# Attention and feed-forward on one core: the list that orders casts, copies, loads, score pieces and feed-forward pieces, written anew

## The chip, the cores and the metric

The kernel runs on one core of one Trainium2 chip. The metric is the time of one execution on the device in microseconds (us), as a median over runs. The profiled execution is a run of its own and has its own time.

## The reference

There are two steps. The first is masked attention for 4 batches, 8 heads, 768 tokens and head size 64. The second is a feed-forward layer on its output.

```python
B, H, S, D = q.shape                      # 4, 8, 768, 64
scores = matmul(q, k.T) / sqrt(D)         # per batch and head
# heads 0, 2, 6 ("retrieval"): causal mask
# heads 1, 3, 4, 5, 7 ("streaming"): causal and (key < 4 or query - key < 64)
a = softmax(where(mask, scores, -1e9)); attn = matmul(a, v)
x = attn.transpose(0, 2, 1, 3).reshape(3072, 512)
h = x @ w_in                              # 512 -> 2048
g = maximum(h, 0) + alpha * minimum(h, 0)
out = g @ w_out                           # 2048 -> 512, float32
```

## The kernel before, in words

The attention is cut into 16 segments n, four to a batch; segment n holds batch n // 4 and the head pair PAIRS[n % 4] of (2, 6), (1, 5), (0, 4), (3, 7). The feed-forward layer is cut into 8 token tiles t, two to a batch: even t has 512 tokens, odd t 256. The feed-forward tiles of batch b need the four segments of that batch, so the kernel alternates: attention of batch 0, feed-forward of tiles 0 and 1 with the attention of batch 1 woven in, and so on.

The order of all work is written out by hand. `ORDER` is a string of 1,076 names; each name is an item, a small function that emits its instructions, and a loop at line 806 calls them in the order of the string. A framework adds the semaphore waits that the data needs, but it moves nothing: every engine and every DMA queue carries out its own instructions strictly in the order in which the string emits them. The names are

- `Lq5`, `Lk5`, `Lv5`: the loads of q, k, v for segment 5, all on the queue of SyncE (SP) except the first half of `Lk0` (ScalarE's queue) and two small pieces of `Lk13` (GpSimd's). One load of a segment is 384 to 448 KB. `load_rows` (line 230) reads v in rows of 256 bytes. Up to segment 7, q comes in rows of 1,536 bytes and k in rows of 512 or 1,536; from segment 8 on both come in rows of 256. The buffers qf, kf, vf have four slots each, so that a load waits for the cast of the segment four before it.
- `wi0` to `wi7` (line 690) and `wo0` to `wo3` (line 695): the loads of w_in (eight pieces) and w_out (four pieces of 1 MB in the source), on GpSimd's queue, which converts them to bf16 on the way.
- `Cq6`, `Ck6.0`, `Cv6`: casts of a loaded tile to bf16. Which engine makes one is fixed by three strings, lines 296 to 298: GpSimd ("P") for v of segments 0 to 5, VectorE ("V") from segment 6 on (both halves of `Cv3` stand apart). `Cv6` is emitted by `cast_v` (line 346, its instruction is at line 348 and writes vb).
- `Tq`, `Tk`, `tq`, `tk`: transposes of q and k on TensorE (to segment 7) and the copies out of PSUM; `Dq`, `Dk`: the same by DMA transpose on SP's queue (from segment 8).
- `S4.0.3`, `s4.0.3`, `m4.0.3`: one piece of the scores on TensorE, its exponential on ScalarE, its mask on VectorE. From segment 4 on, score pieces that follow each other with nothing but light items between them are collected and emitted as one group by `emit_burst`; where both heads of a group have at least 576 columns, the two heads run side by side on the two halves of the array.
- `A4.0`, `a4.0`: scores times v on TensorE and the division on VectorE; `X4`, `x4`: the transpose into xT (by DMA on SP's queue for segments 4 to 14).
- `P0.9` (`P1`, line 588): one piece of x @ w_in in one PSUM bank; `p0.9` (`relu`, line 600) is its negative part on ScalarE into one of three buffers; `g0.9` (`prelu`, line 604) combines the two on VectorE and gives the bank free. `P0.0.0` to `P0.5.2` are the first six pieces of tile 0, cut in three by head pair.
- `O0.1.2`, `o0.1`: a quarter of g @ w_out, and the copy and store of the result (`P2_out`, line 620); `L0` to `L2`, `l0` to `l2`: the last 128 tokens, cut by columns.
- `warm0` to `warm8`: matmuls on a tile of zeros, whose result nobody reads; `busy`, `zero`, `kz`, `qz`, `vz`, `sz`, `so`, `ro`, `nz`, `kfz`, `near`: fills; `id`, `nms`, `nmr`, `nr`, `ns`: the identity and the masks, made on GpSimd.

PSUM has eight banks. An item on TensorE takes one (two for early scores) and the item that reads it last gives it back; `take` (line 144) picks the bank that has been free longest in the order of the string, so the string fixes which item waits for which.

Of the kernel before, what the change touches and what calls it, by code (L numbers as in the profile page):

```python
# [24 lines left out]
p1.12 P0.14 g1.12 p0.14 g0.14 P0.13 p0.13 g0.13 P0.11 p1.14 Tk5 Ck7.1 g1.14 P1.10 tk5.0 p0.11 p1.10 Ck6.0 Ck7.0 g0.11  # L25
m8.0.2 tk5.1 wo2 Lv6 Lv4 P0.10 P0.8 p0.8 Tk7 g1.10 wo3 Cq4 Lk9 P0.12 P1.8 p0.10 g0.8 p0.12 g0.10 Tq4 P0.6 P0.9 p0.3
Ck6.1 g0.3 tq4 P0.4.0 P0.5.0 Tk6 P0.4.1 p1.8 g1.8 tk7.0 p0.9 g0.9 Cq6 P0.5.1 P0.5.2 p0.5 g0.12 p0.6 tk6.1 P0.4.2 g0.6
g0.5 tk6.0 S4.0.5 P0.7 p0.7 P1.6 g0.7 P1.4 s4.0.5 p0.4 Tq6 m4.1.2 tk7.1 g0.4 Cv5 p1.6 g1.6 O0.1.0 tq6 S4.0.3 O0.2.0
O0.2.1 S5.1.1 S5.0.0 S4.0.1 S6.1.0 m14.0.2 p1.4 g1.4 s5.0.0 O0.1.1 s4.0.3 s4.0.1 O0.2.2 S5.0.2 S5.1.0 S4.0.2 S5.1.2
s6.1.0 m4.0.1 Cv7 O0.3.0 s5.0.2 s5.1.2 s5.1.1 s4.0.2 O0.1.2 s5.1.0 O0.1.3 o0.1 Cq7 Cv4 O0.3.1 m5.1.0 m8.1.2 m5.0.2  # L30
m4.0.3 m5.1.2 S4.0.0 S4.1.4 S5.0.1 S4.0.4 S4.1.0 s4.0.4 s5.0.1 Lk10 m5.0.1 O0.2.3 O0.3.2 Tq7 m5.0.0 o0.2 s4.1.0 m4.0.4
m5.1.1 A5.1 s4.0.0 m4.0.0 a5.1 O0.3.3 tq7 S7.0.0 S7.0.1 S4.1.3 S7.1.1 S6.0.5 S4.1.1 m4.0.5 s4.1.4 o0.3 Lq9 s4.1.3 Ck8
m4.1.3 A5.0 a5.0 X5 s4.1.1 A4.0 s7.0.0 s7.1.1 Lk11 Lq8 s7.0.1 a4.0 s6.0.5 near1 m7.0.0 m7.1.1 m4.1.0 O1.1.0 S7.1.0
S6.0.4 S7.0.2 S4.1.5 S6.0.1 S7.1.2 S6.1.1 O1.1.1 Cv6 s7.1.0 O1.0.0 s4.1.5 m7.0.1 s6.1.1 m4.1.5 m6.1.1 s7.1.2 m6.1.0
# [812 lines left out]
```

## Time and profile before

| | |
|---|---|
| median of 3 runs | 229.18 us (229.06 to 229.55) |
| the profiled execution | 229.83 us, span 228.0 us |
| TensorE busy | 222.4 us, 98% of the span |
| VectorE, ScalarE, GpSimd busy | 151.6, 139.6, 45.8 us |
| DMA packets | 95,417; 82,440 of them under 512 bytes |
| first and last matmul start | 1.07 and 224.87 us |

The span runs from the first to the last instruction of the program on the core; 1.83 us of the execution lie around it. All times inside the kernel are counted from the span's start. Among the groups of instructions, each matmul of the feed-forward layer is listed with a modelled length (326 and 379 ns in the mean); what one costs is read from the distance between starts in the time line, 0.216 us for 512 columns and 0.109 us for 256.

### The profile page before, as it was taken

The page shows a single profiled execution, that of the slowest core. Times are in us where ns is not written, and L with a number is a line of the kernel's source. Part 1 is how long each engine was busy: PE and PEld are TensorE (multiplying, and loading weights), DVE is VectorE, ACT ScalarE, POOL GpSimd, SP SyncE. Part 2 cuts the span into 40 slices and gives each one's busy share as a digit, 9 for nine tenths or more (in the row PEclk, how much of TensorE's full clock was granted, in tenths as well). Part 3 has the DMA queues.
Part 4 walks back from the last instruction along what each step waited for, and adds up shares of the span by engine and source line. Part 5 has one row for each costly group of instructions (what it writes and reads, how often), then busy time and mean ns, then how long its engine had stood idle before and what let it go on. Part 6 is the DMA issues. An engine that isn't in the chain of part 4 may idle for free.

```text
span 228.0 us, 5239 instructions
## 1 busy us (share of the span) xinstructions
PE 222.4 (98%) x2005; PEld 135.9 (60%) x2005; DVE 151.6 (66%) x395; ACT 139.6 (61%) x284; POOL 45.8 (20%) x91
## 2 busy tenths in 40 slices
...
DMA  6999999999998798989969899995821420000213
GB/s 190 313 229 210 286 223 262 206 197 241 206 287 142 132 204 227 172 192 181 254 153 199 194 266 146 218 166 107 132 93 38 116 95 0 0 4 0 88 66 123
DMA packets 95417, 37.39 MB, mean 164 GB/s; under 512 B 82440, under 2 KB 93600, under 8 KB 95392
## 3 DMA queue, kind: packets, MB, share of 16 engines
...
q14 instruction: 10, 0.08, 0.2%
...
## 4 chain that ended last, share of the span: by engine, by line
PE 92%; ACT 3%; DVE 2%; issue 1%; DVEq 0%; ACTq 0%
PE P L597 35%; PE P L617 34%; PE P L552 7%; PE P L430 4%; PE P L687 3%; PE P L413 2%; PE P L363 2%; PE P L636 2%; ACT neg L602 1%; PE P L501 1%; DVE kT L392 1%; PE P L423 1%; PE P L577 1%; ACT kT L392 1%; ACT eS L523 1%
## 5 line engine op out<-in xcount | busy, mean ns | idle before, releaser
L609 DVE SCALAR_TENSOR_TENSOR g<-neg,oma,P 128x256 bf16<-128x256 f32 (+1 forms) x128 | 71.0, 608 | 35.9 <-ACT neg L602 35.5
L597 PE MATMUL P<-xT,w_in_b 128*128 128x512 bf16 (+1 forms) x512 | 86.5, 326 | 0.0
L617 PE MATMUL P<-w_out_b,g 128*128 128x512 bf16 x368 | 85.4, 379 | 0.0
L602 ACT ACTIVATE neg<-P 128x512 f32<-128x512 f32 x96 | 54.4, 600 | 27.2 <-PE P L597 22.6
L597 PEld LDWEIGHTS <-w_in_b 128*128 128x128 bf16 x512 | 49.5, 98 | 31.7 <-DVE g L609 0.2
L617 PEld LDWEIGHTS <-g 128*128 128x128 bf16 x368 | 33.8, 98 | 37.2 <-issue 1.2
L469 ACT ACTIVATE eR<-P 128x448 bf16<-128x448 f32 (+4 forms) x63 | 37.1, 636 | 5.4 <-PE P L430 2.3
L623 ACT COPY ot<-P 128x512 f32<-128x512 f32 x23 | 13.8, 602 | 37.8 <-PE P L617 32.9
L627 POOL DMA_DIRECT2D out_dram<-ot x18 | 10.3, 571 | 113.2 <-ACT ot L623 113.0
L517 ACT ACTIVATE eS<-P 128x352 bf16<-128x352 f32 x45 | 21.0, 493 | 3.7 <-PE P L430 3.7
L563 DVE TENSOR_TENSOR xn<-P,rcp 128x448 bf16<-128x448 f32 (+1 forms) x32 | 19.5, 608 | 1.1
L528 DVE TENSOR_TENSOR eS<-eS,ms_near 128x352 bf16<-128x352 bf16 x45 | 14.3, 334 | 4.4 <-ACT eS L517 4.2
L479 DVE TENSOR_TENSOR eR<-eR,mr_near 128x128 bf16<-128x128 bf16 (+5 forms) x54 | 12.1, 252 | 4.0 <-ACT eR L469 4.0
L430 PE MATMUL P<-qT,kT 64*128 64x176 bf16 (+13 forms) x181 | 11.7, 251 | 0.3 <-DVE g L609 0.3
L430 PEld LDWEIGHTS <-kT 64*128 64x128 bf16 x181 | 7.2, 94 | 7.6 <-issue 6.8
L413 PE MATMUL P<-qT,kT 128*128 128x192 bf16 (+14 forms) x68 | 11.3, 251 | 0.3 <-ACT eS L523 0.3
L552 PE MATMUL P<-vb,eS 128*128 128x65 bf16 x260 | 11.0, 193 | 0.4 <-DVE eS L528 0.4
L552 PEld LDWEIGHTS <-eS 128*128 128x128 bf16 x260 | 9.7, 97 | 2.9 <-DVE eS L528 0.6
L562 DVE RECIPROCAL rcp<-P 128x7 f32<-128x7 f32 (+1 forms) x32 | 6.3, 198 | 7.1 <-PE P L552 6.9
L552 PE MATMUL P<-vb,eR 128*128 128x65 bf16 x276 | 10.1, 192 | 0.0
L552 PEld LDWEIGHTS <-eR 128*128 128x128 bf16 x276 | 9.4, 97 | 1.2
L645 DVE COPY ot<-P 128x128 f32<-128x128 f32 x1 | 0.3, 292 | 14.3 <-PE P L636 14.3
...
## 6 DMA issues: line engine op xcount, KB each, us to landing
...
w_out_b<-in_moe_w_out_dram POOLq DMA_DIRECT2D x4, 512.0 KB, 13.4
```

The costliest lines, as they stand in the source:

```text
L413: nc.tensor.matmul(to, keys, queries, start=True, stop=stop)
L430: nc.tensor.matmul(to, keys[own], queries[own], start=True, stop=True)
L469: nc.scalar.activation(ebuf[n, hh][:, lo:hi].rearrange("p (x c) -> p x c", x=len(parts)), P[:, got[0]:got[0] + len(parts), 0:(hi - lo) // ...
L517: nc.scalar.activation(slots, sc[:, 0:352].rearrange("p (s c) -> p s c", c=176), AF.Exp, scale=scale)
L528: nc.vector.tensor_tensor(slots, slots, ms_near[:, 0:2, :] if m == 0 else ms_near[:, 1:3, :], op=ALU.mult)
L552: nc.tensor.matmul(pav[:, i, :], e[:, o:o + 128], vv[:, j, hh, 0:D + 1], start=(m == 0), stop=(m == len(terms) - 1))
L563: nc.vector.tensor_tensor(xn[n][:, 0:nt, D * hh:D * hh + D], pav[:, :, 0:D], rcp.to_broadcast([128, nt, D]), op=ALU.mult)
L597: nc.tensor.matmul(psg[:, w * i:w * (i + 1)], w_in_b[:, c, 128 * fb:128 * (fb + 1)], xT[:, c, o:o + w], start=(x == 0), stop=(x == 3))
L602: nc.scalar.activation(neg[t, f], bank(held["P", t, f][0]), AF.Relu, scale=-1.0)
L609: nc.vector.scalar_tensor_tensor(g_buf[t % 2][:, fb, 0:w], neg[t, f][:, c], oma[:, fb:fb + 1], bank(got[0])[:, c], op0=ALU.mult, op1=ALU.add)
L617: nc.tensor.matmul(bank(held["O", t, s][0]), g_buf[t % 2][:, f, 128 * s:128 * (s + 1)], w_out_b[:, f, :], start=(f == 0), stop=(f == 15))
L623: nc.scalar.copy(ot, bank(got[0]))
```

## The change

Only the string `ORDER` changes. It holds the same 1,076 names, each once, in another order; no function, buffer or constant is touched, and each engine carries out the same number of instructions. Casts, copies, fills, masks, score pieces and feed-forward pieces stand in other places. The sequence of w_in and w_out on GpSimd's queue is the same (1, 0, 6, 7, 5, 4, 2, 3, then w_out). On SP's queue the first fourteen loads keep their sequence up to `Lq5`; from there on it is another: before `Lk4 Lk5 Lk7 Lk6 Lq4 Lq6 Lv7 Lv5 Lq7 Lk8 Lv6 Lv4`, after `Lv4 Lk4 Lk5 Lq7 Lk7 Lk6 Lq4 Lv6 Lq9 Lq6 Lv7 Lk8 Lv10 Lv5`. On VectorE, `Cv6` stands before between `m4.1.0` and `m7.0.1` (in the time line it runs at 69.3 us), and after directly behind `x3`, ahead of `near0` and `g1.2`.

The string's beginning, up to the first half of the feed-forward of batch 0, and its end:

```diff
-busy zero La id warm0 kz3 Lq0.0 sz1 vz2 nms nmr so1 vz0 Lq0.1 Lk1 warm8 warm5 warm3 kz1 qz0 one Lq1 Lk0 Ck0.0 Cq0.0
...
-Lk3 S0.1.0 kfz0 Lv1 vo ro0 Ck3.1 s0.1.0 Lq3 Ck3.0 wi1 wi0 Cq3 sz0 S1.0.0 so2 Al s1.0.0 so0 al S0.1.1 s0.1.1 Lv2 Tq2
...
-X0 s2.0.1 x0 wi6 s2.0.2 wi7 Lv3 Lq5 Tq3 tk3.1 S2.0.0 wi5 m4.0.2 warm6 S2.1.0 A1.0 a1.0 Lk4 s2.0.0 A2.0 S2.1.1 A1.1
-a2.0 tq3 s2.1.0 a1.1 S3.0.0 s2.1.1 s3.0.0 A2.1 a2.1 S3.1.1 X1 S3.0.1 s3.0.1 Lk5 wi4 kfz2 Cv3.0 Cq5 Lk7 wi2 X2 Ck4.0
-s3.1.1 S3.1.0 x1 P0.0.0 x2 P0.0.1 A3.0 P0.1.0 P0.1.1 Lk6 Lq4 Lq6 Ck4.1 kfz3 nr Cv3.1 s3.1.0 A3.1 Lv7 Lv5 Lq7 Ck5.0 wi3
-a3.0 P0.2.0 Tq5 tq5 P0.3.0 P0.3.1 a3.1 X3 x3 ns kfz1 P0.2.1 Tk4 near2 P1.2 P0.1.2 P0.2.2 P0.0.2 p1.2 p0.1 g0.1 Ck5.1
-P1.0 P0.3.2 g1.2 P0.15 tk4.0 p0.2 g0.2 p0.15 wo0 p1.0 Lk8 near0 g0.15 g1.0 ro1 P1.12 P1.14 m12.1.2 p0.0 g0.0 wo1 tk4.1
...
-m12.0.2 g7.14 L2 l2 O7.0.3 o7.0 L0 L1 l1 warm1 l0
+busy zero nms one warm6 Lq0.0 id Lq0.1 sz2 kfz0 warm0 ro0 kz1 kz0 Lk1 Lq1 idf La Lk0 Cq0.0 vz3 wi1 Tq0.0 qz0 sz1 so1
...
+Tq0.1 Lv0 Lq2 Lk3 Tq1 S0.0.2 s0.0.0 tk1.0 tq1 warm3 Ck0.1 tq0.1 Tk0.1 tk0.1 Ck2.1 kz2 wi0 s0.0.2 so2 S1.1.0 warm4
...
+s0.1.2 Tq2 tq2 A0.0 a0.0 S1.0.1 A0.1 a0.1 s1.0.1 so0 S1.1.1 wi6 wi7 s1.1.1 S2.0.1 s2.0.1 Lv2 Lv3 Ck3.1 Lq5 Ck3.0 Tk3
+tk3.0 Lv4 Cv1 S2.0.0 s2.0.0 A1.0 a1.0 S2.0.2 Cq3 s2.0.2 X0 x0 Tq3 tq3 tk3.1 S2.1.0 Lk4 Lk5 s2.1.0 Lq7 Cv2 A2.0 a2.0
+wi5 A1.1 a1.1 Lk7 wi4 S2.1.1 s2.1.1 S3.0.0 s3.0.0 nr Lk6 Lq4 A2.1 Cv3.0 S3.0.1 a2.1 nz0 X1 x1 Ck4.0 s3.0.1 S3.1.0 A3.0
+S3.1.1 kfz3 ro1 X2 s3.1.0 Lv6 Cv3.1 P0.1.0 x2 P0.3.0 P0.2.0 s3.1.1 Cq5 A3.1 P0.1.1 P0.0.0 Tq5 a3.0 P0.0.1 a3.1 X3
+Ck4.1 Tk4 tk4.0 tk4.1 P0.2.1 kfz2 x3 P1.2 p1.2 wi2 Lq9 P0.2.2 Lq6 P0.0.2 P0.3.1 P0.3.2 P0.1.2 Cv6 Lv7 p0.3 near0 p0.2
+g1.2 near1 P1.0 g0.2 wi3 Ck5.0 g0.3 P1.12 p0.1 P1.14 p1.12 wo0 P0.13 tq5 wo1 wo2 wo3 g1.12 p1.0 g1.0 Lk8 p0.13 g0.13
+P0.15 Ck5.1 Tk5 p1.14 tk5.0 P1.8 p1.8 g0.1 g1.14 g1.8 P0.9 p0.9 Ck7.0 Cq4 g0.9 p0.0 g0.0 P0.14 Lv10 tk5.1 P0.8 p0.8
...
+O6.0.2 o6.1 O6.0.3 o6.0 L2 L0 L1 l2 o6.2 warm1 l0 l1
```

More of the change, by code (lines that the diff above doesn't have):

```diff
@@ L25 @@
[L25 to L34, printed above, removed]
@@ L70 @@
[L70 removed]
+busy zero nms one warm6 Lq0.0 id Lq0.1 sz2 kfz0 warm0 ro0 kz1 kz0 Lk1 Lq1 idf La Lk0 Cq0.0 vz3 wi1 Tq0.0 qz0 sz1 so1
+vz1 vz0 warm7 vz2 nmr Ck1.0 Ck0.0 Tk0.0 sz0 warm2 tk0.0 Ck1.1 Tk1 tk1.1 tq0.0 S0.0.1 s0.0.1 Cq0.1 warm5 S0.0.0 Cq1 Lk2
+Tq0.1 Lv0 Lq2 Lk3 Tq1 S0.0.2 s0.0.0 tk1.0 tq1 warm3 Ck0.1 tq0.1 Tk0.1 tk0.1 Ck2.1 kz2 wi0 s0.0.2 so2 S1.1.0 warm4
+S0.1.0 s1.1.0 S1.0.0 Ck2.0 Tk2 s0.1.0 tk2.0 s1.0.0 Al S0.1.1 s0.1.1 vo warm8 qz Lv1 Lq3 Cv0 kz3 al S0.1.2 Cq2 tk2.1
@@ new lines @@
+g1.2 near1 P1.0 g0.2 wi3 Ck5.0 g0.3 P1.12 p0.1 P1.14 p1.12 wo0 P0.13 tq5 wo1 wo2 wo3 g1.12 p1.0 g1.0 Lk8 p0.13 g0.13
+P0.15 Ck5.1 Tk5 p1.14 tk5.0 P1.8 p1.8 g0.1 g1.14 g1.8 P0.9 p0.9 Ck7.0 Cq4 g0.9 p0.0 g0.0 P0.14 Lv10 tk5.1 P0.8 p0.8
+P0.11 g0.8 m4.1.2 P1.10 P0.4.0 p0.14 P0.4.1 p0.15 g0.15 P0.12 Ck6.1 p1.10 g1.10 Tq4 p0.11 tq4 P0.4.2 p0.4 g0.11 P0.6
+p0.6 P0.10 S4.0.3 Ck6.0 g0.14 P0.5.0 Tk6 g0.4 S4.0.5 Cq6 m14.0.2 p0.12 s4.0.5 kfz1 s4.0.3 P0.5.1 P0.5.2 p0.5 g0.12 Lv5
+P0.7 p0.7 g0.6 Tq6 tq6 g0.5 g0.7 Lk9 m4.0.3 p0.10 O0.2.0 tk6.1 tk6.0 P1.4 O0.2.1 p1.4 Ck7.1 Tk7 g0.10 near2 Ck8 ns
@@ new lines @@
+tk7.0 P1.6 S4.0.1 Lq8 g1.4 S5.1.1 S6.1.0 S5.0.0 O0.2.2 s4.0.1 nz1 Cv4 Cq7 O0.1.0 O0.1.1 p1.6 g1.6 O0.2.3 s5.1.1 m5.1.1
+Tq7 Cv5 tk7.1 S5.0.1 s5.0.0 m5.0.0 S5.1.2 S4.0.2 s6.1.0 S5.1.0 tq7 O0.1.2 s5.0.1 O0.1.3 s5.1.0 Cq8 s5.1.2 m5.1.2
+m8.1.2 s4.0.2 o0.1 O0.3.0 S4.1.0 S4.0.0 S4.1.4 S4.0.4 o0.2 Lk11 S7.1.1 S5.0.2 Cv7 O0.3.1 m5.1.0 s4.1.0 m12.1.2 A5.1
+s4.1.4 Lq10 O0.3.2 O0.3.3 m5.0.1 Lv9 s4.0.0 Ck9 m4.0.0 S6.0.5 S4.1.3 m8.0.2 s7.1.1 m4.1.4 m4.0.1 a5.1 S7.0.0 s5.0.2
+S6.1.1 s4.0.4 o0.3 S4.1.1 S7.0.1 Lq11 m4.0.4 Lk10 Dk8.0 m5.0.2 A5.0 s4.1.3 m4.0.5 A4.0 s7.0.0 a5.0 s4.1.1 a4.0 O1.1.0
@@ new lines @@
+s7.0.1 m7.0.1 S6.0.4 s6.1.1 S7.1.0 S7.0.2 S6.0.1 m7.1.1 S4.1.5 m6.1.1 S7.1.2 s6.0.5 Dk9.1 s7.1.0 Dk9.0 s4.1.5 m4.1.5
+m4.1.0 s6.0.4 m6.0.5 O1.0.0 m6.0.4 O1.1.1 s7.1.2 S6.1.2 S4.1.2 m4.1.1 S6.0.3 m7.1.0 m7.1.2 S6.0.0 X5 m6.1.0 s7.0.2
+m7.0.2 O1.1.2 s6.0.1 m7.0.0 O1.1.3 s4.1.2 S6.0.2 Dq8 m4.1.3 s6.0.0 m6.0.0 A4.1 m6.0.1 s6.1.2 m6.1.2 s6.0.3 m6.0.3 o1.1
+a4.1 X4 A7.0 A6.1 a6.1 s6.0.2 A6.0 A7.1 O0.0.0 O0.0.1 O0.0.2 m6.0.2 a6.0 S8.0.0 O1.0.1 O1.0.2 O1.0.3 a7.0 O0.0.3 a7.1
+o1.0 S8.0.5 Cq9 s8.0.5 m8.0.5 S8.0.1 s8.0.1 o0.0 X6 Cq10 X7 P2.10 Dq9 P3.14 Lq12 P2.8 Cv9 Cq11 S9.0.0 p2.10 Ck11 P3.4
@@ new lines @@
+P3.2 g2.10 p3.14 g3.14 s9.0.0 P2.9 Dk8.1 Dq11 s8.0.0 m9.0.0 p3.4 Lv11 p3.2 g3.2 p2.9 P2.6 S9.0.2 g2.9 P2.3 p2.8 g2.8
+P2.2 p2.6 g2.6 g3.4 p2.2 g2.2 P2.5 P2.11 p2.11 g2.11 P3.6 Ck10 p3.6 g3.6 S9.0.1 s9.0.1 p2.5 Lk12 p2.3 g2.3 Cv11 P2.12
+p2.12 g2.12 P2.4 P3.10 p2.4 g2.4 P2.0 p2.0 g2.0 P2.1 p2.1 s9.0.2 S9.1.0 g2.1 Lk13 P2.14 m8.0.1 s9.1.0 p3.10 g3.10
+P2.15 P3.0 Dq10 g2.5 S9.1.1 Cq12 p2.14 P2.7 p2.7 g2.7 P2.13 p2.13 g2.13 s9.1.1 g2.14 O2.0.0 O2.0.1 Lq13 p3.0 m8.0.0
+Dk10.1 g3.0 O2.0.2 p2.15 Cq13 Lq15 S8.1.5 s8.1.5 m8.1.5 P3.8 p3.8 S8.1.3 S8.0.3 S8.0.4 S8.1.4 Dk10.0 g2.15 g3.8 P3.12
@@ new lines @@
+s8.1.4 p3.12 m8.1.4 s8.0.4 g3.12 Dk11.1 m8.0.4 m9.1.0 O2.0.3 o2.0 s8.0.3 s8.1.3 Dk11.0 O3.0.0 O3.0.1 S11.0.1 S10.1.2
+S11.0.2 S10.1.0 S9.1.2 S8.0.2 S11.0.0 Lv8 Cv8 s9.1.2 Lv15 m9.1.1 Cv10 m8.0.3 s10.1.2 m9.1.2 O3.0.2 m9.0.1 s10.1.0
+O3.0.3 m9.0.2 A9.0 o3.0 Dq13 s8.0.2 s11.0.0 m8.1.3 a9.0 A9.1 a9.1 O2.3.0 O2.3.1 S10.0.3 s11.0.2 S10.1.1 S8.1.1 S10.0.1
+m10.1.0 m11.0.0 S8.1.0 s11.0.1 S10.0.0 S8.1.2 s10.1.1 Lk14 Ck13 A8.0 s8.1.1 m8.1.1 Dq12 s8.1.0 m10.1.1 a8.0 m11.0.1
+O2.3.2 s10.0.1 m8.1.0 m10.0.1 s10.0.0 m10.1.2 Lv13 s10.0.3 Ck12 O2.3.3 O3.1.0 m11.0.2 S10.0.4 s8.1.2 S10.0.5 S11.1.2
@@ new lines @@
+o2.3 S11.1.0 S11.1.1 S10.0.2 s11.1.0 m11.1.0 A10.1 a10.1 Dk13.0 s10.0.4 X9 s10.0.5 m10.0.5 s10.0.2 m10.0.3 O3.1.1
+m10.0.4 m10.0.0 A8.1 Dk13.1 O3.1.2 a8.1 A10.0 s11.1.1 m11.1.1 O3.1.3 s11.1.2 m11.1.2 A11.1 A11.0 a10.0 m12.0.2 X10
+O2.2.0 S13.0.1 a11.0 X8 O2.2.1 O2.2.2 O2.1.0 O2.1.1 Cq15 O2.1.2 O2.1.3 O2.2.3 a11.1 X11 P4.12 p4.12 Dk12.0 g4.12 P4.6
+p4.6 g4.6 s13.0.1 o3.1 P4.2 p4.2 g4.2 S12.0.5 s12.0.5 P4.10 P5.2 p4.10 P5.0 Dk12.1 p5.2 S12.0.3 s12.0.3 o2.2 Lq14 Cq14
+P4.13 p4.13 g5.2 P5.12 p5.12 g4.10 Lk15 o2.1 g5.12 P4.4 P5.14 p4.4 g4.4 P4.0 p5.0 g4.13 P4.1 Dq14 p5.14 P4.9 g5.14
@@ new lines @@
+P4.11 p4.1 p4.9 g5.0 P4.8 Lv12 g4.1 P4.3 g4.9 m12.0.3 p4.11 g4.11 S12.1.5 S12.0.0 S12.0.1 p4.8 g4.8 m4.0.2 p4.3
+S13.1.1 g4.3 p4.0 g4.0 P4.7 Ck14 s12.0.0 m12.0.0 Dk14.0 s13.1.1 m13.1.1 Dk14.1 s12.1.5 m13.0.1 P5.4 p5.4 P5.6 g5.4
+P4.15 P4.5 p4.7 p5.6 P4.14 p4.14 g4.7 O4.3.0 O5.1.0 p4.5 Dq15 Ck15 g5.6 g4.14 P5.10 s12.0.1 p4.15 P5.8 m12.0.1 S13.1.0
+S12.0.4 g4.5 p5.10 g4.15 g5.10 S12.0.2 S12.1.1 p5.8 g5.8 O4.3.1 Lv14 s13.1.0 Cv12 O4.3.2 O4.3.3 s12.0.4 Cv13 s12.1.1
+s12.0.2 o4.3 S14.0.0 S14.0.1 S14.1.0 S14.1.1 S13.0.2 S12.1.4 O5.1.1 s14.1.0 s13.0.2 s14.1.1 s12.1.4 m12.0.5 m12.0.4
@@ new lines @@
+A12.0 s14.0.1 s14.0.0 O4.2.0 O4.2.1 m14.1.1 a12.0 S13.0.0 m13.0.2 S14.0.4 S13.1.2 m12.1.1 S14.1.2 S12.1.2 S14.0.5
+Dk15.0 O5.1.2 Cv14 s12.1.2 s13.1.2 m13.1.2 m10.0.2 O4.2.2 s14.1.2 O4.2.3 m14.1.2 O5.1.3 S15.0.0 s13.0.0 S14.0.3
+S12.1.0 S12.1.3 Dk15.1 s14.0.4 s14.0.5 m13.0.0 o4.2 m14.1.0 A13.0 s12.1.3 O5.0.0 s12.1.0 a13.0 s14.0.3 m12.1.4 O5.0.1
+m14.0.1 S15.1.1 S15.1.0 S15.0.2 S14.0.2 m13.1.0 s15.0.0 S15.0.1 S15.1.2 Cv15 o5.1 s14.0.2 s15.0.2 O5.0.2 A13.1 s15.1.0
+m12.1.0 s15.1.1 m12.1.5 m14.0.0 s15.0.1 m12.1.3 m14.0.4 A12.1 O4.0.0 O4.0.1 m15.0.2 m14.0.5 a12.1 X12 m14.0.3 a13.1
@@ new lines @@
+X13 A14.0 m15.1.0 A14.1 m15.0.1 s15.1.2 m15.1.2 O5.0.3 a14.0 o5.0 O4.0.2 O4.0.3 o4.0 m15.0.0 A15.0 a14.1 m15.1.1 X14
+A15.1 O4.1.0 a15.0 O4.1.1 O4.1.2 a15.1 X15 O4.1.3 x15 o4.1 P6.0 P6.4 P6.15 p6.15 P6.12 P6.3 p6.3 g6.15 p6.0 g6.0 g6.3
+P6.2 p6.2 P7.2 p6.4 g6.4 P6.5 P6.1 P6.7 P7.6 p6.1 g6.1 g6.2 p7.2 g7.2 P6.9 p6.9 g6.9 p6.12 g6.12 P7.0 P7.4 P6.6 p7.6
+p6.5 P6.10 g6.5 g7.6 P7.12 p6.7 P6.13 p7.4 p6.10 g7.4 g6.10 p7.0 g7.0 P7.10 p6.13 P6.8 P6.14 g6.7 g6.13 p6.8 O7.0.0
+p7.12 g6.8 p6.6 P7.8 p7.10 P7.14 g6.6 O7.0.1 O6.3.0 O6.3.1 p6.14 g6.14 O6.2.0 O6.2.1 g7.12 P6.11 p6.11 g6.11 O6.1.0
```

39 lines of the change are left out of this document (1 added, 38 removed).

## The prediction

> **What bounds the kernel now.** First the page: how busy is each engine, and how busy are the DMA engines over the 40 slices (5.7 us each)?
>
> ```profile
> PE 222.4 (98%) x2005; PEld 135.9 (60%) x2005; DVE 151.6 (66%) x395; ACT 139.6 (61%) x284; POOL 45.8 (20%) x91
> ...
> DMA  6999999999998798989969899995821420000213
> ```
>
> TensorE works nearly all the time, so the kernel before has little left to gain: what TensorE must do costs the same in both orders. The DMA engines are just as full until about 165 us. Next the waits: who stood still for a load?
>
> ```profile
> PE P L687 <- DVE zero L288: 1.1, 1, 1.1
> ...
> POOL vb L348 <- DMA vf<-in_v_dram: 16.3, 2, 15.0
> ```
>
> Only GpSimd waits long for a load, and nobody waits for GpSimd: TensorE's longest wait is the first us. The time line of GpSimd shows which loads are late:
>
> ```profile
> 34.80 3.01 POOL L696 DMA_DIRECT2D w_out_b<-in_moe_w_out_dram  x4
> 40.58 0.83 POOL L315 CAST natq<-qf 128x768 bf16<-128x768 f32 x1 [2.77 <-DMA qf<-in_q_dram]
> 56.37 0.93 POOL L348 CAST vb<-vf 128x896 bf16<-128x896 f32 x1 [14.97 <-DMA vf<-in_v_dram]
> ```
>
> These are `wo0` to `wo3`, `Cq4` and `Cv5`. `Lq4` lands at 40.5 us; the next three loads on SP's queue, `Lq6`, `Lv7` and `Lv5`, need until 56.3 us. That is the cost of the weights beside them, which land late themselves (the tile view of w_out_b):
>
> ```profile
> DMA to landing us min/median/max: 9.5/13.4/17.4
> ```
>
> The last of the four is issued at 37.0 us, so it lands at 54.4 us. In the trace's packet records the two queues alternate one to one in this stretch: from 44 to 52 us 1,254 packets of weights and 1,253 rows of the loads started, 156 each per us. With the weights gone, from 56 to 64 us, 6,220 rows of 256 bytes started, 777 per us. So while weights are queued, a v load of some 1,600 rows takes 10 us, and 2 us without them.
>
> Last, VectorE at the beginning of the feed-forward:
>
> ```profile
> 30.70 0.56 DVE L582 COPY xT<-P 128x768 bf16<-128x768 bf16 x1 [0.94 <-PE P L577]
> 31.21 0.10 DVE L681 MEMSET eS<- 128x48 f32 x1
> 31.27 0.09 DVE L682 MEMSET eS<- 128x32 f32 x1
> 33.24 2.19 DVE L609 SCALAR_TENSOR_TENSOR g<-neg,oma,P 128x512 bf16<-128x512 f32 x4 [1.89 <-ACT neg L602]
> ```
>
> After `x3` and a fill come the g items, which give PSUM banks back. No load is among them.
>
> **The change, part by part.** *The large part: `Cv6` on VectorE.* In the changed order VectorE has `x3`, `Cv6`, `near0`, `g1.2`, and then all other g items. `Cv6` needs `Lv6`, and VectorE is in order, so no bank of the feed-forward comes free before `Lv6` has landed. On SP's queue `Lv6` stands directly behind `Lq4`, with `Lv4` and `Lq7` newly ahead of it. `Lq4` landed at 40.5 us with fewer rows ahead of it, so `Lv6` must come later than that, but VectorE reaches `Cv6` at about 32 us.
>
> When does `Lv6` land? GpSimd issues `wi2`, `wi3` when `Lk4` has landed and `wo0` to `wo3` when half of `Lk5` has. From there `Lq7`, `Lk7`, `Lk6`, `Lq4` and `Lv6` are left, some 2,700 to 3,100 rows, against 6 pieces with 2,560 packets of weights. At one to one, all weights pass before the last rows of `Lv6`. So I count what the DMA engines have done by then. Before, all weights and the loads through `Lv7` had landed at 54.4 us. After, all weights and the loads through `Lv6` are the same rows, but for `Lv4`, `Lq7`, `Lv6` (1,536 + 256 + 1,580) in place of `Lq6`, `Lv7` (256 + 1,624): 1,492 rows more, at 777 per us 1.9 us. About 1 us comes back, because `wi1` is issued near 3 us instead of 16.2 us, when the DMA slice is 6. `Lv6` lands at 55.5 us. Bounds: 51.5 us if the weights start 2 us late and fewer rows share with them, 58 us if the early weights hold up the first loads and nothing comes back.
>
> What stops meanwhile? TensorE goes on until it has no bank. By the banks that the order assigns, the four pieces of tile 0, `Tq5` (its copy `tq5` stands on ScalarE behind `p1.12`, which needs one of the three neg buffers, so a g), `P1.2`, `P1.0` and `P1.12` take all eight, and `P1.14` takes that of `P1.2`: it waits for `g1.2`. So `P1.14` starts at 55.5 + 0.62 (`Cv6`, row of the same cast on VectorE) + 0.15 (`near0`, two fills) + 0.86 (two halves of g, row at 40.14 us) = 57.1 us. Before it started at 35.39 us: **+21.7 us**. How late TensorE gets there is no matter, as long as it is before 57 us: the startup, where loads are late by the early `wi1` and `wi0` (each 256 packets beside them, 1 to 1.5 us), is covered by the hold. Without this cover it would cost 1 to 3 us.
>
> *What is left behind `P1.14`.* The same matmuls, but `P0.15` now stands behind it, not ahead: +0.9 us (4 x 0.216). *Score groups:* the groups of before come to 24,512 columns, counting heads side by side once, those of after to 25,272, since more pieces stand alone (`S8.0.0`, `S9.0.0` among others): 760 columns at 2,400 per us, +0.3 us. *The wait in `A5.1`* (0.61 us at 64 us, for the mask of segment 5) falls away: these masks stand further ahead, -0.6 us.
>
> *The clock behind a long gap.* The first 44 matmuls on zeros cost 107 ns each, from 1.07 to 5.9 us, the same matmuls later 56 ns: half speed at the start, 2.3 us lost, though the row of the granted clock shows a 9 throughout. Whether 20 us of idling bring this back no row of before shows; the bounds are 0 and 2.3 us, and I take **+2.3**, since the only idle TensorE in the trace was followed by it. [...]
>
> *Parts that cost nothing.* Fills and masks that move on VectorE and GpSimd: GpSimd idles 15 us at `Cv5` before, and what VectorE does ahead of `Cv6` is covered by the hold; without it each costs its row, 0.1 to 0.9 us. Later loads, `Dq`, `Dk`, `X` in new places on SP's queue: TensorE needs them 20 us later, while the queue, free of weights, still moves 777 rows per us; `Lv5`, 8,000 rows further back than before, lands near 67 us and `A5.1` now comes near 85 us. If that cover were gone (no hold), `Lv5` alone would hold TensorE some 5 us. At the end `o6.2` is stored behind `L2`, ahead of `l1` on SP's queue; a store of that size lands 2.0 us after its issue and `l1` is issued over 1 us behind it: 0 to 0.3 us, taken as 0.
>
> Sum: 21.7 + 0.9 + 0.3 - 0.6 + 2.3 = 24.6 us. Against the profiled execution's own time that is 229.83 + 24.6 = 254.4 us (span 228.0 to 252.6, with the same 1.83 us around it); that execution lay 0.65 us above the median, so **253.8 us**.
>
> **The rivals.** *The weights do not stand in the way of `Lv6`.* If GpSimd issued `wi2` onward only when `Lv6` is through, the 2,560 packets would not share with it; one to one they take 17 us, in which the rows that pass would alone take about 5.5. `Lv6` lands at 44 us, time 242.3 us. For it: GpSimd has much to do ahead of `wi2`. Against: it waits there only for `Lk4` and `Lk5`, 8 us of unshared rows ahead of `Lv6`. Chance 0.08.
>
> *`Lv6` is in time, and the order gains.* It decides at 33.5 us: with `Lv6` landed by then, `g1.2` is done when TensorE comes to `P1.14`. What remains is -0.6 (`A5.1`), some -1.0 (waits of 0.63 and 0.33 us at 10.9 and 12.9 us in the startup) and +0.3: 227.9 us. Against it: `Lq4`, ahead of `Lv6`, lands at 40.5 us before. Chance 0.04.
>
> *It holds longer.* The first loads are 3 us late, `Lv6` lands at 60 us, and VectorE and ScalarE, at 0.7 and 0.6 us per bank, are slow to clear eight banks at half clock: 259 to 262 us. Chance 0.04.
>
> That the change does not do what it says is plain, and no rival: its words keep the sequence of the loads, the built queue of SP does not. Had it been kept, `Lv6` would land at 61.5 us as before, and the hold be longer still.
>
> **How the numbers follow.** The hold with a landing between 51.5 and 58 us: 0.84. Its low end is 51.5 without the clock's loss, 253.8 - 4.0 - 2.3 = 247.5 us; its high end 253.8 + 2.5 + 1, about 257.5 us. The range reaches down to 244 us, for landings between this and the first rival, and up to 258 us. Less than 0.2% either way (0.46 us) can't be told from no change. Faster 0.04, same 0.01, slower 0.95.
>
> **What would show it.** Right: on VectorE a cast vb<-vf of 0.62 us at 55 to 56 us, with over 20 us of idling before it that a DMA of vf ends; TensorE idle from about 36 to 57 us in front of a 256-column matmul, then matmuls at twice their length for some us; `Cv5` on GpSimd without its 15 us of waiting ahead of TensorE's need; the stretch behind `P1.14` as long as before but for 3 us. Wrong: `Cv6` before 45 us, or TensorE at work through the hold, because the banks are others than I counted; or a second gap of several us, at `A5.1`, `P2` or `P4`.

## The result, and the profile after

The changed kernel takes **255.3 us** (median of four runs, 254.3 to 257.3) against 229.4 us for the kernel before beside it (229.1 to 229.9): ratio 1.114, 95% interval 1.107 to 1.121. Four further runs, among the experiments, gave 255.4 us and 1.109 (1.103 to 1.116). The forecast was slower, 253.8 us, with a range of 244 to 258. Here and below, runs more than 1.5% above the fastest of their own kernel do not enter the ratios.

The page of the profiled execution (255.34 us, span 253.6 us) shows the hole: in the rows of 40 slices (6.3 us each) TensorE stands at 0 for two slices, and the granted clock (PEclk, in tenths of full speed) shows three fives.

```profile
PE 225.8 (89%) x2005; PEld 138.0 (54%) x2005; DVE 152.1 (60%) x395; ACT 139.8 (55%) x284; POOL 46.3 (18%) x91
...
PE   8976794006999999999999999999999999999995
...
PEclk9999799555999999999999999999999999999999
```

TensorE is busy for 3.4 us more than before, but in a span that is 25.6 us longer. The list of waits (us in total, how often, the longest) names the chain:

```profile
DVE vb L348 <- DMA vf<-in_v_dram: 20.5, 1, 20.5
ACT neg L602 <- DVE eS L682: 19.1, 1, 19.1
...
PE P L597 <- DVE g L609: 18.4, 1, 18.4
```

VectorE, ScalarE and TensorE stand still at once, and of these three only VectorE waits for a load: ScalarE and TensorE wait for VectorE. VectorE's time line has the cast and what comes behind it, TensorE's the end of the hold (the time in which it stands still):

```profile
57.73 0.63 DVE L348 CAST vb<-vf 128x896 bf16<-128x896 f32 x1 [20.52 <-DMA vf<-in_v_dram]
58.32 0.10 DVE L681 MEMSET eS<- 128x48 f32 x1
58.37 0.45 DVE L609 SCALAR_TENSOR_TENSOR g<-neg,oma,P 128x256 bf16<-128x256 f32 x1
58.37 0.09 DVE L682 MEMSET eS<- 128x32 f32 x1
58.73 0.48 DVE L609 SCALAR_TENSOR_TENSOR g<-neg,oma,P 128x256 bf16<-128x256 f32 x1
```

```profile
36.78 4.08 PE L597 MATMUL P<-xT,w_in_b 128*128 128x512 bf16 x30
59.26 4.91 PE L597 MATMUL P<-xT,w_in_b 128*128 128x256 bf16 x16 [18.40 <-DVE g L609]
64.00 0.50 PE L363 MATMUL P<-ident,natm 128*128 128x128 bf16 x6
```

`Lv6` lands at 57.5 us, then come `Cv6`, `near0`, the two halves of `g1.2` and, at 59.26 us, `P1.14`. The last line is `Tk5`: the three items `P1.14`, `P0.13` and `P0.15`, 2.6 us of work at full speed, took 4.74 us. The chain of work that ended last goes through the same load:

```profile
37.81 19.73 DMA vf<-in_v_dram
59.26 4.91 PE P L597 x16
```

The whole difference can be laid out on one start. Before, `P1.14` started at 35.39 us, inside a run of feed-forward matmuls without a wait:

```profile
31.05 6.25 PE L597 MATMUL P<-xT,w_in_b 128*128 128x256 bf16 x44
```

Now it starts at 59.26 us: +23.9 us. From there to the end of the span it takes 194.3 instead of 192.6 us: +1.7. The time around the span is 0.1 us less. Sum: 25.5 us, the distance between the two profiled executions. Behind `P1.14` TensorE has no second gap: no wait there is as long as 0.2 us.

The startup is later, too. TensorE waits 3.2 us for `Cv2`, which GpSimd can begin only at 25.9 us, when `Lv2` has landed:

```profile
PE P L552 <- POOL vb L348: 3.7, 2, 3.2
```

At `A2.0` (26.87 us) TensorE is 10.5 us behind the sum of its own work up to there, counted at full speed; before it was 5.1. The hold hides this, as the prediction said it would, but there was more to hide.

### The profile page after: what moved, and what is told of

It reads as the page before. It is cut to its first block, busy times and chain, and to the rows that moved or that the text cites. A ratio compares the mean times of both kernels' runs of the same rounds, so it can differ in the third digit from the quotient of the medians.

```text
span 253.6 us, 5239 instructions
## 1 busy us (share of the span) xinstructions
PE 225.8 (89%) x2005; PEld 138.0 (54%) x2005; DVE 152.1 (60%) x395; ACT 139.8 (55%) x284; POOL 46.3 (18%) x91
## 3 DMA queue, kind: packets, MB, share of 16 engines
q0 software_dynamic: 5792, 8.93, 16.1%
## 4 chain that ended last, share of the span: by engine, by line
PE 79%; DMA 14%; SPq 2%; DVE 1%; POOL 1%; issue 0%; ACT 0%; DVEq 0%
PE P L617 32%; PE P L597 31%; DMA vf<-in_v_dram 11%; PE P L552 5%; DMA kf<-in_k_dram 4%; PE P L430 4%; PE P L687 2%; PE P L636 1%; SPq L209 1%; PE P L363 1%; PE P L423 1%; SPq L223 1%; SPq L246 1%; PE P L361 0%; PE P L413 0%
## 5 line engine op out<-in xcount | busy, mean ns | idle before, releaser
L597 PE MATMUL P<-xT,w_in_b 128*128 128x256 bf16 (+1 forms) x512 | 89.7, 331 | 18.4 <-DVE g L609 18.4
L609 DVE SCALAR_TENSOR_TENSOR g<-neg,oma,P 128x512 bf16<-128x512 f32 (+1 forms) x128 | 72.2, 609 | 29.2 <-ACT neg L602 28.3
L469 ACT ACTIVATE eR<-P 128x448 bf16<-128x448 f32 (+4 forms) x63 | 36.2, 620 | 7.9 <-PE P L462 3.3
L623 ACT COPY ot<-P 128x512 f32<-128x512 f32 x23 | 13.5, 599 | 26.1 <-PE P L617 22.6
L517 ACT ACTIVATE eS<-P 128x352 bf16<-128x352 f32 x45 | 20.0, 476 | 2.8 <-PE P L430 2.1
L563 DVE TENSOR_TENSOR xn<-P,rcp 128x448 bf16<-128x448 f32 (+1 forms) x32 | 19.5, 608 | 1.9 <-DMA xT<-xn 0.8
L348 DVE CAST vb<-vf 128x896 bf16<-128x896 f32 x10 | 6.1, 622 | 20.5 <-DMA vf<-in_v_dram 20.5
L479 DVE TENSOR_TENSOR eR<-eR,mr_near 128x128 bf16<-128x128 bf16 (+5 forms) x54 | 10.1, 227 | 7.1 <-ACT eR L469 7.0
L552 PE MATMUL P<-vb,eR 128*128 128x65 bf16 x276 | 10.9, 197 | 3.3 <-POOL vb L348 3.2
L552 PEld LDWEIGHTS <-eR 128*128 128x128 bf16 x276 | 10.2, 100 | 4.8 <-issue 3.7
L430 PE MATMUL P<-qT,kT 64*128 64x176 bf16 (+11 forms) x170 | 10.9, 252 | 0.0
L523 ACT ACTIVATE eS<-P 128x768 bf16<-128x768 f32 (+1 forms) x10 | 6.4, 653 | 6.7 <-PE P L501 6.5
```

The source lines that it names most:

```text
L430: nc.tensor.matmul(to, keys[own], queries[own], start=True, stop=True)
L469: nc.scalar.activation(ebuf[n, hh][:, lo:hi].rearrange("p (x c) -> p x c", x=len(parts)), P[:, got[0]:got[0] + len(parts), 0:(hi - lo) // ...
L517: nc.scalar.activation(slots, sc[:, 0:352].rearrange("p (s c) -> p s c", c=176), AF.Exp, scale=scale)
L552: nc.tensor.matmul(pav[:, i, :], e[:, o:o + 128], vv[:, j, hh, 0:D + 1], start=(m == 0), stop=(m == len(terms) - 1))
L563: nc.vector.tensor_tensor(xn[n][:, 0:nt, D * hh:D * hh + D], pav[:, :, 0:D], rcp.to_broadcast([128, nt, D]), op=ALU.mult)
L597: nc.tensor.matmul(psg[:, w * i:w * (i + 1)], w_in_b[:, c, 128 * fb:128 * (fb + 1)], xT[:, c, o:o + w], start=(x == 0), stop=(x == 3))
```

## Experiments

Two theories stood against each other at first. A: every engine carries out its items in order, so a cast that waits for a late load holds everything behind it, and `Cv6` is only the first of several such casts. B: this one wait is the whole loss. The expectations add C, that the early weights are the cause, and later D, that the queue of SP as a whole is late because of the weights beside it.

**Cv6 taken out of the way.** `Cv6` back to its place of before, the load that reuses its buffer behind it.

```diff
-... P0.1.2 Cv6 Lv7 p0.3 near0 p0.2 g1.2 ... P0.14 Lv10 tk5.1 ... m4.1.0 s6.0.4
+... P0.1.2 Lv7 p0.3 near0 p0.2 g1.2 ... P0.14 tk5.1 ... m4.1.0 Cv6 Lv10 s6.0.4
```

> The changed order with Cv6 moved back to its old neighbourhood (behind m4.1.0) and Lv10, which reuses its slot, behind it; all else as changed. If the wait of VectorE for Lv6 is the first of several in-order waits (theory A), VectorE frees banks again at once, and the next engine to stand is ScalarE at Cq6: Lq6 lands near 60 us as in the changed kernel, so Tq6 starts near 62 us and TensorE, some 6 us late from the startup, runs dry for about 7 us: 243.5 us (241 to 246). If that one wait is all there is to lose (theory B), only the late startup is left: 229.4 + 6 = 235.5 us or less. If the early weights are the cause (theory C), nothing comes back: 254 to 256 us.

Measured: 245.2 us (ratio 1.067, 1.065 to 1.070). The hold at `P1.14` is gone, and another one stands further on: TensorE is idle from about 55 us until `Tq6` at 63.6 us, for `Lq6`, whose cast `Cq6` is on ScalarE (list of waits):

```profile
ACT natq L315 <- DMA qf<-in_q_dram: 9.0, 1, 9.0
...
PE P L363 <- ACT eR L469: 8.5, 1, 8.5
```

A holds; B falls, and so does C as the whole cause. `Cv6`'s wait of 20.5 us is worth 10 us in the time, since its hold covered the late startup and the wait for `Lq6`.

**Cv6 at the same place, on GpSimd.** The letter of the engine for cast 6 is changed.

```diff
-    CV = "PPPPPPVVVVVVVVVV"
+    CV = "PPPPPPPVVVVVVVVV"
```

> The changed order with Cv6 cast on GpSimd instead of VectorE. VectorE is then free, and GpSimd, which waits in Cv6 instead, issues wi3 and wo0 to wo3 only behind it: so the weights do not share with Lv6. Theory A: Lv6 lands at 42 to 45 us instead of 57.5, since up to 2,300 weight packets no longer pass beside it; the weights land until about 61 us, Lq6 lands at 55 to 58 us beside them, and Cq6 on ScalarE holds TensorE there: 238 us (235 to 242). If the landing of Lv6 does not depend on the weights beside it, it lands at 55 us or later and wi3 and the w_out pieces come so late that the time is 250 us or more.

Measured: 246.5 us (1.074, 1.069 to 1.079), 8 us over what A expected. GpSimd's time line says why:

```profile
46.89 0.93 POOL L348 CAST vb<-vf 128x896 bf16<-128x896 f32 x1 [11.02 <-DMA vf<-in_v_dram]
47.76 0.61 POOL L692 DMA_DIRECT2D w_in_b<-in_moe_w_in_dram  x1
48.37 0.52 POOL L328 CAST natm<-kf 128x384 bf16<-128x384 f32 x1
48.81 3.02 POOL L696 DMA_DIRECT2D w_out_b<-in_moe_w_out_dram  x4
51.80 0.55 POOL L328 CAST natm<-kf 128x384 bf16<-128x384 f32 x1
```

Behind `Cv6` on GpSimd stand `wi3`, `Ck5.0`, the issues of `wo0` to `wo3` and `Ck5.1`, and TensorE waits 7.9 us for `Ck5.1` at `Tk5` (52.4 us). I had not looked at what is queued behind the wait on the new engine. The run answers something else as well: with `wi3` and all of w_out issued only behind `Lv6`, `Lv6` landed at 46.7 us instead of 57.5. That is the mechanism of the prediction's first rival (44 us there): it is in large part the weights beside it that make `Lv6` late.

**The change's one step alone, in the kernel before.** `Lv6` directly behind `Lq4`, `Cv6` directly behind `x3`, all else as before.

```diff
-... Lk6 Lq4 Lq6 ... X3 x3 ns ... wo2 Lv6 Lv4 ... Cv6 s7.1.0
+... Lk6 Lq4 Lv6 Lq6 ... X3 x3 Cv6 ns ... wo2 Lv4 ... s7.1.0
```

> The order of before with two names moved: Lv6 directly behind Lq4 on SP's queue, Cv6 directly behind x3 on VectorE, as in the changed kernel; all other loads and the weights as before. Theory A: Lq4 lands at 40.5 us, the 1,580 rows of Lv6 at 156 per us take 10 us more, so Lv6 lands at 51 us, g0.1 ends at 52.5 us and P1.12 starts there instead of at 34.5 us; with 2 us for the halved clock 249 us (246 to 252). Theories B' (the other loads in new places) and C (the early weights) leave it at 230 to 231 us.

Measured: 248.95 us in the median, 244.6 to 249.8 in four runs (too wide for a ratio). Two moved names make the kernel before 15 to 20 us slower, through the same two waits:

```profile
DVE vb L348 <- DMA vf<-in_v_dram: 18.7, 1, 18.7
...
PE P L597 <- DVE g L609: 16.7, 1, 16.7
```

**The weights late again.** The changed order with `wi1`, `wi0` behind `Ck3.0` and `wi6`, `wi7` behind `Cv2`.

```diff
-... vz3 wi1 Tq0.0 ... kz2 wi0 s0.0.2 ... S1.1.1 wi6 wi7 s1.1.1 ... Ck3.0 Tk3 ... Cv2 A2.0
+... vz3 Tq0.0 ... kz2 s0.0.2 ... S1.1.1 s1.1.1 ... Ck3.0 wi1 wi0 Tk3 ... Cv2 wi6 wi7 A2.0
```

> The changed order with wi1, wi0 behind Ck3.0 and wi6, wi7 behind Cv2 on GpSimd, about where they stand before. Theory A: the startup is 4 to 6 us earlier (the last matmuls ahead of the gap end near 36 us instead of 41), but the same rows pass until Lv6 has landed, 56 to 58 us, and the hold covers it: 253 to 256 us. Theory C: the time falls by the 6 us of the startup, to 249 us.

Measured: 250.3 us, 247.4 to 255.1 (1.081, 1.076 to 1.086). The startup is as before (5.1 us behind at `A2.0`), the hold is still there, and in the profiled run (251.8 us) it ends 3.5 us sooner, with the start of `P1.14` at 55.73 instead of 59.26 us:

```profile
PE P L597 <- DVE g L609: 16.4, 1, 16.4
```

`Lv6` landed at 54.1 us instead of 57.5, `wo3` at 55.7 instead of 57.8. From `P1.14` to the end of the span it is 194.3 us, as in the changed kernel. Neither theory is right: C had the time nearly, but not its reason, and A had the hold, but not where it ends. The prediction's estimate that early weights bring `Lv6` forward by 1 us seems to have the wrong sign. One landing does not show it, since two runs further down, with early weights, have 54.5 and 56.3 us; the times do better: the median is 5 us lower, and none of eight runs of the changed kernel took less than 253.8 us, and three of these four did.

**One wait after the other.** The kernel without `Cv6`'s wait, with `Lq6` directly behind `Lq4`; then the same with late weights; then with the late loads `Lq7`, `Lv5`, `Lk8`, `Lv7`, `Lv4`, `Lv6` in this sequence and `Ck8`, `Cv4`, `Cv7` behind them.

```diff
-... Lk6 Lq4 A2.1 ... P0.2.2 Lq6 P0.0.2
+... Lk6 Lq4 Lq6 A2.1 ... P0.2.2 P0.0.2
```

> The changed order with Cv6 late (as in the run with Cv6 behind m4.1.0) and Lq6 on SP's queue directly behind Lq4. Theory A (a chain of in-order waits: whichever load stands last decides): that run still stood still for 9.1 us at Tq6, from about 54.5 to 63.6 us, because Cq6 on ScalarE waited for Lq6, which landed at 61.7 us. With Lq6 ahead of Lv6 it lands before 50 us; the standstill goes, and the half clock behind it with some 1.5 to 2 us: 245.2 - 9.1 - 1.7 = 234.5 us (233 to 238), of which some 6 us are the late startup. Theory D (SP's queue as a whole is late, the weights beside it decide): the standstill only moves to the next load, Lv7 or Lv5, and 240 to 244 us remain.

```diff
-... vz3 wi1 Tq0.0 ... kz2 wi0 s0.0.2 ... S1.1.1 wi6 wi7 s1.1.1 ... Ck3.0 Tk3 ... Cv2 A2.0
+... vz3 Tq0.0 ... kz2 s0.0.2 ... S1.1.1 s1.1.1 ... Ck3.0 wi1 wi0 Tk3 ... Cv2 wi6 wi7 A2.0
```

> As the run with Lq6 behind Lq4 and Cv6 late, and in addition wi1 and wi0 issued behind Ck3.0, wi6 and wi7 behind Cv2. Theory A: nothing covers the startup any more, so the weights now count with the whole of what they cost there, about 6 us (TensorE was 11.7 us behind its own work at S3.0.0 against 5.1 us before): 234.5 - 6 = 228.5 us. Lv5 landed at 66.4 us with late weights and Cv5 ends a us later, while A5.1 would come at 64 to 65 us: 2 to 3 us may come back there. 231 us (228.5 to 234). If the early weights cost only the 1 to 3 us of the prediction: 232 to 235 us.

```diff
-Lq5 Lv4 Lk4 Lk5 Lq7 Lk7 Lk6 Lq4 Lq6 Lv6 Lq9 Lv7 Lk8 Lv5
+Lq5 Lk4 Lk5 Lk7 Lk6 Lq4 Lq6 Lq7 Lv5 Lk8 Lv7 Lv4 Lv6 Lq9
-... Ck8 ns ... nz1 Cv4 Cq7 ... Tq7 Cv5 ... Lk11 S7.1.1 S5.0.2 Cv7 ... O0.3.3 m5.0.1 ... a5.1 S7.0.0
+... ns ... nz1 Cq7 ... Tq7 Ck8 Cv5 ... Lk11 S7.1.1 S5.0.2 ... O0.3.3 Cv4 m5.0.1 ... a5.1 Cv7 S7.0.0
```

> The changed order, in which only loads, weights and the casts behind them are moved: wi1, wi0, wi6, wi7 late as before; on SP's queue Lk4 Lk5 Lk7 Lk6 Lq4 Lq6 Lq7 Lv5 Lk8 Lv7 Lv4 Lv6; and the casts set behind the time at which these loads can land: Ck8 behind Tq7, Cv4 behind O0.3.3, Cv7 behind a5.1, Cv6 behind m4.1.0. All other items stay in the changed order. If the whole loss comes from loads that land later than an in-order engine's cast wants them, nothing of the 26 us is left: 229.4 us + 0.3 (score groups) - 0.6 (wait of A5.1) = 229 us (228 to 231.5; the upper end if Lv5, at 56 us, or Lk8 still holds somebody for a us or two). If the other items' new places cost something of their own, it stays above 232 us.

Measured: 242.5 us (1.054, 1.049 to 1.059), 241.6 (1.053, 1.049 to 1.056) and 241.5 (1.054, 1.049 to 1.059). My expectation failed all three times, by 8 to 12.5 us, and D held in the first, though the load was another than it named: the standstill moved on each time. First to `Lk8`, whose cast `Ck8` on VectorE stands ahead of g items that `O0.2.2` needs (list of waits of the first, whose profiled run took 244.8 us):

```profile
DVE natk L334 <- DMA kf<-in_k_dram: 7.4, 1, 7.4
...
PE P L617 <- DVE g L609: 6.1, 1, 6.1
```

With late weights the startup was back to 5.0 us behind, and TensorE stood still at `Tq5`, for `Cq5`, which is queued on GpSimd behind the cast of the first half of `Lk4` (it landed at 34.2 us with `Lv4` ahead of it, and at 27.2 us in the third of these runs, without). The last line is `Ck8` again:

```profile
POOL natm L328 <- DMA kf<-in_k_dram: 7.7, 1, 7.7
...
PE P L363 <- POOL natq L315: 6.4, 1, 6.4
DVE natk L334 <- DMA kf<-in_k_dram: 4.0, 1, 4.0
```

In the third, TensorE is hardly later than before up to `P0.4.0` (43.4 us; 6.2 us behind its own work, before 5.7 at the same amount of work), so that startup, `Cv6` and `Lk8` cost next to nothing any more. What is left are smaller waits: 2.0 us for `Lq4` at `Tq4`, then 3.4 us for `Cq8` on VectorE, which waits for `Lq8` ahead of the masks of `A5.1`, then 3.3 us near 88 us, for VectorE, which waits there for a transpose by DMA (xT from xn) on SP's queue:

```profile
46.39 0.51 PE L363 MATMUL P<-ident,natq 128*128 128x128 bf16 x6 [1.99 <-POOL natq L315]
69.70 0.57 PE L552 MATMUL P<-vb,eS 128*128 128x65 bf16 x13 [3.45 <-DVE eS L528]
```

```profile
68.46 0.56 DVE L315 CAST natq<-qf 128x768 bf16<-128x768 f32 x1 [6.68 <-DMA qf<-in_q_dram]
```

These waits are 8.7 us. Behind the first and the last the granted clock is at half for 3.4 us, from 47.2 and from 88.2 us, which costs some 1.7 and 1.6 us (an estimate, half of the time in which TensorE works there). Together that is 12.0 of the 12.5 us that this kernel takes more than the kernel before. So the new places of the other items cost little of their own here, but they decide which load is wanted early, and no run shows them without these waits. What is shown: each time a wait for a load was taken away, another cast with a late load held the next engine, and at last a transpose on the same queue.

**The sequence of the loads as the change's words have it.** The changed order, SP's queue in the sequence of before.

```diff
-Lq5 Lv4 Lk4 Lk5 Lq7 Lk7 Lk6 Lq4 Lv6 Lq9 Lq6 Lv7 Lk8 Lv10 Lv5
+Lq5 Lk4 Lk5 Lk7 Lk6 Lq4 Lq6 Lv7 Lv5 Lq7 Lk8 Lv6 Lv4 Lq9 Lv10
```

> The changed order with the sequence of the loads of before on SP's queue (Lk4 Lk5 Lk7 Lk6 Lq4 Lq6 Lv7 Lv5 Lq7 Lk8 Lv6 Lv4), all casts and weights where the changed order has them. By the chain of waits Cv6 decides alone, and Lv6 now stands behind Lq6, Lv7, Lv5, Lq7 and Lk8: it landed at 61.5 us in the trace of before and, with the startup late, lands at 62 to 66 us. P1.14 starts 1.8 us behind that, at 66 us instead of 59.3: 255.3 + 6.5 = 262 us (259 to 265). If the sequence on the queue is what costs the time, and not Cv6's place, the time falls well below 250 us.

Measured: 262.0 us (1.142, 1.136 to 1.148), to the number. `Lv6` landed at 63.5 us. So it is the place of `Cv6` that costs the time; the new sequence of the loads makes its hold shorter:

```profile
DVE vb L348 <- DMA vf<-in_v_dram: 26.2, 1, 26.2
...
PE P L597 <- DVE g L609: 24.1, 1, 24.1
```

**The half clock by itself.** TensorE is kept busy through the hold: `P1.12` is carried out 21 times into its own bank.

```diff
+        rep = 21 if (t, f) == (1, 12) else 1
-        for i, fb in enumerate(range(f, f + 512 // w)):
+        for i, fb in [z for _ in range(rep) for z in enumerate(range(f, f + 512 // w))]:
```

> The changed order, in which the 16 matmuls of P1.12 are carried out 21 times, each time from the start into the same bank, so that TensorE is busy from 41 to about 58.5 us while it waits for the bank of P1.14. Nothing else changes: p1.12 on ScalarE waits for a neg buffer through the same stretch. If the half clock behind the idle time costs what the traces say (TensorE fell back another 2.1 us between 59.3 and 64 us), the granted clock stays at 1.00 from 40 us on and the time is 255.3 - 2.1 = 253.2 us (252 to 254.3), with P1.14 still at 59 us. If the slow matmuls there had another cause (the banks, the g items), the time stays at 255.3 us (254.5 to 256).

Measured: 252.5 us (1.101, 1.097 to 1.105), 2.8 us below the changed kernel. Behind the hold the clock stays full (the 7 is the stretch behind the wait for `Cv2`):

```profile
PEclk9999799999999999999999999999999999999999
```

`Tk5` starts at 61.10 us here, and from there to the end of the span it is 189.6 us, the same as in the changed kernel (253.6 - 64.00). The two part ahead of `Tk5`: 2.1 us are the matmuls at half speed, the rest, 0.8 us, is an earlier start of `P1.14` (`Lv6` landed at 54.5 us, but TensorE was held by the repeats until about 58.5).

**The early weights by themselves.** The kernel before, only `wi1`, `wi0`, `wi6`, `wi7` earlier.

```diff
-... Cq0.0 Tq0.0 ... Ck2.1 tq1 ... Cv0 Lk3 ... Ck3.0 wi1 wi0 Cq3 ... x0 wi6 s2.0.2 wi7 Lv3
+... Cq0.0 wi1 Tq0.0 ... Ck2.1 wi0 tq1 ... Cv0 wi6 wi7 Lk3 ... Ck3.0 Cq3 ... x0 s2.0.2 Lv3
```

> The kernel before, in which only wi1, wi0, wi6 and wi7 are issued earlier, about where the changed order has them: wi1 ahead of Tq0.0, wi0 behind Ck2.1, wi6 and wi7 behind Cv0. The prediction put the startup's delay by the early weights, without the hold that covers it, at 1 to 3 us: 230.4 to 232.4 us. The traces since say some 6 us (TensorE at S3.0.0 was 11.7 us behind its own work in the changed kernel, 5.1 before and 5.1 with the changed order and late weights): 234 to 236 us, with Cv1 and Cv2 on GpSimd waiting for Lv1 and Lv2, and TensorE for them at A1 and A2.

Measured: 236.7 us, +7.0 us (1.032, 1.024 to 1.039). In TensorE's time line the first two of these waits are new; the third line is `S3.1.0`, which started at 25.95 us before:

```profile
16.77 1.45 PE L363 MATMUL P<-ident,g 128*128 128x128 bf16 x12 [2.07 <-POOL g L315]
27.62 0.97 PE L552 MATMUL P<-vb,eR 128*128 128x65 bf16 x27 [1.99 <-POOL vb L348]
32.09 0.24 PE L413 MATMUL P<-qT,kT 128*128 128x192 bf16 x1 [0.18 <-ACT eS L523]
```

`Lv1` landed at 20.1 us instead of 16.1, `Lv2` at 26.5 instead of 19.5. Behind the first of the waits the granted clock is at half from 16.8 to 20.2 us, some 1.7 us lost (an estimate, half of that stretch). The time is just above what the traces had led me to expect, and far above the 230.4 to 232.4 us of the prediction.

**How far the landing varies.** The changed kernel once more.

> The changed kernel once more, unaltered, for a second trace. The prediction had Lv6 at 55.5 us and the first trace has it at 57.5; in two experiments with the same loads up to Lv6 it landed at 54.3 and 54.5 us. If the landing varies by this much from run to run, a second trace gives anything from 54 to 58 us, the start of P1.14 follows it by 1.7 us, the time moves with it, 252.5 to 256 us, and the stretch from P1.14 to the end stays at 194.3 us. If the 2 us are a steady error of the prediction's count, Lv6 lands at 57 to 58 us again.

Measured: 255.4 us, 253.8 to 257.7. The profiled run (253.82 us) has `Lv6` at 56.3 us and

```profile
57.97 4.69 PE L597 MATMUL P<-xT,w_in_b 128*128 128x256 bf16 x16 [16.82 <-DVE g L609]
```

From there to the end of the span (252.1 us) it is 194.1 us, as in the first trace (194.3). The landing moves by a us or more from run to run (with 54.5 us in the run with the repeats by up to 3), and the time moves with it.

**A version that might beat both.** The kernel before with `O0.3.3` ahead of `A5.1`, to cover the wait for a mask there.

```diff
-... A5.1 s4.0.0 m4.0.0 a5.1 O0.3.3 tq7
+... O0.3.3 A5.1 s4.0.0 m4.0.0 a5.1 tq7
```

> The kernel before with one name moved: O0.3.3 ahead of A5.1. A5.1 waited 0.61 us for a mask at 64 us; O0.3.3 (4 matmuls of 0.22 us) needs nothing that is late there. If the wait is real, 229.2 - 0.6 = 228.6 us (228.5 to 229.0). If what stands behind only waits later for the same mask or exponential, 229.2 us.

Measured: 229.7 us (1.002, 1.000 to 1.004): nothing gained. The wait at `A5.1` is gone, and a new one stands 1.5 us behind it:

```profile
66.21 0.37 PE L430 MATMUL P<-qT,kT 64*128 64x280 bf16 x4 [0.50 <-DVE xn L563]
```

VectorE has the same work to do by then, and is now waited for at the next place. No version that I ran beats the kernel before.

## Why the prediction was right, step by step

**The mechanism was right in each link.** The cast on VectorE with 20.5 us of idling before it, the bank of `P1.2` that `P1.14` waits for, ScalarE and TensorE held behind VectorE: all are in the trace as forecast. Two moved names in the kernel before make most of the loss; the unaltered sequence of the loads makes the hold longer, as the prediction said in passing (262.0 us).

**The landing of `Lv6`, 55.5 us, was 0.8 to 2 us early** (56.3 and 57.5 in the two traces), and so was the large term: +21.7 forecast, +22.6 and +23.9 measured. The run with the repeats, with the same loads, had 54.5 us, so the forecast lies inside what one kernel shows. The step that failed is "about 1 us comes back, because `wi1` is issued near 3 us". With late weights all weights landed at 55.7 us, 1.3 us later than before, where the prediction had 1.9 for the additional rows; with early weights at 57.5 and 57.8, and at 58.4 in the run with the repeats. The early weights found little idle DMA time (from 3 to 5 us the busy share of the DMA engines was 0.92 before and 0.98 after), they delayed the first loads, and GpSimd's later issues with them (`wo0` at 36.2 us; before at 34.8, with late weights at 35.0).

**The startup's 1 to 3 us were 6 to 7.** The prediction counted what 256 packets beside a load cost that load, for two pieces. It left out that `wi6` and `wi7` come early as well (at 16.5 and 17.1 us instead of 22.1 and 22.7), that the loads queue behind each other, and the half clock behind a wait of 2 to 3 us (3.4 us at 0.50, from 26.1 us, behind the wait of 3.2 us in the changed kernel): `Lv2` came 6 us late in the changed kernel and 7 with the early weights alone, and `Cv2` and TensorE with it. VectorE came to `Cv6` at 37.2 us instead of about 32, and TensorE ran dry at 40.9 instead of about 36. This did little harm to the sum, because the hold covered it: with late weights TensorE was 5.4 us less late at `A2.0`, but the profiled run (251.8 us) only 3.5 us shorter, and all of this is the earlier end of the hold.

**Behind `P1.14`: +2.9 forecast, +1.7 measured.** The half clock was sized well: +2.3 taken, 2.1 found, shown by the repeated `P1.12`. The other three terms came to +0.6 and measured -0.4; the two were not told apart further. The -0.6 for `A5.1` rested on a wait that, taken away alone, came back next door. That the forecast came within 1.5 us is in part luck: the term ahead of `P1.14` was 2.2 us too small, the terms behind it 1.2 us too large.

Behind `P1.14` the granted clock stayed at half for 4.4 us in the first trace of the changed kernel (59.26 to 63.6 us) and for 3.9 us in the second (57.97 to 61.9 us). At work all the time at half speed, TensorE loses half of that, 2.2 and 2.0 us (an estimate), near the 2.1 us found. In the first trace TensorE was busy for 3.40 of the 3.40 us from 60.2 to 63.6 us, still at a granted clock of 0.50, and then the clock was full (0.99 from 63.6 to 67.0 us).

**What the prediction would have got wrong without the hold.** It named `Lv5` as the load that would hold TensorE next, with 5 us. In the runs it was `Lq6` (9.0 us, the wait of the engine that casts), then `Lk8` (7.4 us) or `Lk4` (7.7 us), then `Lq8` (6.7 us). The new sequence sets `Lv6` and `Lq9` newly ahead of `Lq6` and `Lk8`, and `Lv4` ahead of `Lk4`; the casts `Ck8` and `Cq8` stand 74 and 132 names further ahead in the string than before. `Lv5` kept GpSimd waiting (16.2 us in the run without `Cv6`'s wait), but not TensorE.
